# Output layers of a chunked-attention and max-of-three kernel: weights stationary and tokens moving, results stored transposed

## The chip, the cores and the metric

One core of one Trainium2 chip runs the whole program. The metric is the device time of one execution in microseconds (us). TensorE does the matrix products; it holds a stationary operand (128 x 128 in the layers here) and streams a moving operand of 256, 384 or 512 columns through it, adding into PSUM. VectorE (DVE), ScalarE (ACT) and GpSimd (POOL) do the rest, and SyncE (SP) issues every DMA.

## The reference

```python
q, k, v: (8, 8, 576, 64)                       # batch, heads, tokens, width
# attention inside chunks of 64 tokens
scores = (q_c @ k_c^T) / 8
attn = softmax(scores)                          # with 1e-9 added to the sum
x = (attn @ v_c) laid out as (4608, 512)        # tokens by heads*width
h = maximum(maximum(x @ w1, x @ w2), x @ w3)    # w1, w2, w3: (512, 768)
return h @ w_out                                # w_out: (768, 512), result (4608, 512) float32
```

## The kernel before

The 4608 tokens are 36 tiles of 128. Tiles 0 to 7 form two groups of four that are computed plainly; the other 28 are four units of 6, 8, 8 and 6 tiles (`UNITS`, called unit 0 to 3 here). Within a unit, both the hidden layer and the output layer use a seven-product scheme over two-by-two blocks (as Strassen's and Winograd's): products are numbered 1 to 7, and are chained in PSUM as x (1, 6, 5, 3), y (7, 4) and z (2).

Every product in near-float32 precision is three float32r matmuls, `three` (L185 to L188): the stationary and the moving operand are each split into a high and a low half, and it issues low x high, high x low, high x high into one PSUM region. Halves are made by a ScalarE copy (high) and a VectorE subtraction (low). H holds them for the hidden values of a unit (L583 and L586), X for its inputs (L516 and L520).

In the hidden layer (`product`, `hidden`) weights of 128 x 128 from the rings are stationary, and half of the unit's tokens (`half`, 384 or 512 columns) move. The hidden layer goes through nine sets (three pairs of feature blocks by w1, w2, w3). The set's third product is put off into the following set, and that of the last set into the unit's output stage.

The output stage is `project`. For each product in the order `OUT`, and for each of three pairs of feature blocks (`jp`), it goes through the tokens in tiles of 128: the tile's H is stationary, and 256 output columns of the weights move. A PSUM bank takes two tiles of 256 columns. With 3 tiles in half of a 6-tile unit, one bank holds two tiles and a second one holds one. When a product's chain has a result, it is copied aside on ScalarE (L708), added to a kept part on VectorE and stored (L712, L702), or copied on ScalarE and stored (L710, L702). The stores go from four rotating buffers `ao`. Each H is split two products ahead of its use, from within the loop.

The order of the work is written out by a planner: steps of TensorE are yielded one by one with an assumed duration (`OUT_STEP` 0.36 us for three matmuls of 256 columns, `STEP_H` 0.517 or 0.6815 us for three of 384 or 512), and everything else is put into a queue of due times by `plan`, and issued when the assumed clock has passed its time. This fixes the order in which each engine's queue gets its instructions. The inputs X of the next unit are mixed and split (`operands`) from the end of the hidden layer on, at due times that don't depend on the steps of the output stage: behind a 6-tile unit at 9.0 us from the stage's start plus 3.2 us times the entries of `when`, of which 5.0 belongs to `high(3)`. At the ends of products 5 and 4, SyncE is given loads of the next unit's weights.

Of the kernel before, what the change touches and what calls it, by code (L numbers as in the profile page):

```python
# [9 lines left out]
F32 = mybir.dt.float32  # L10
# [9 lines left out]
B, H, S, D = 8, 8, 576, 64  # L20
P = 128
NT = B * S // P
DM, DF, DO = 512, 768, 512
CT, JT = DM // P, DF // P
SCALE = 1.0 / float(D) ** 0.5
GROUPS = [4, 4]
# [6 lines left out]
PAIR_T = (("T", 10.0, 12.4, 0.46), ("at", 10.9, 13.3, 0.0))  # L33
PAIR_D = (("bt", 8.6, 10.5, 0.0), ("bw", 9.6, 11.5, 0.0), ("br", 14.6, 15.6, 0.0))
OUT = (1, 2, 6, 7, 5, 4, 3)
OUT_STEP = 0.36
MIX = 0.5


# [25 lines left out]
def chunk_attn_maxout_kernel(  # L65
# [10 lines left out]
    nc = tc.nc  # L76
# [8 lines left out]
    ao_p = ctx.enter_context(tc.tile_pool(name="ao_p", bufs=1))  # L85
# [15 lines left out]
    def take():  # L101
        assert banks, "no bank is free"
        pool, tag = place = banks.pop(0)
        if not kept_until_read:
            banks.append(place)
        return pool.tile([P, 512], F32, name="pm", tag=tag), place

    def give(place):
        assert kept_until_read
        banks.append(place)  # L110

    ident = small.tile([P, P], F32, name="ident")
    make_identity(nc, ident)

# [11 lines left out]
    for name in FIRST.split():  # L126
        k = (3 * int(name[1]) + int(name[2])) if name[0] in "WAXY" else None
# [57 lines left out]
    def three(o, ah, al, bh, bl, first, last, shared=False):  # L185
        nc.tensor.matmul(out=o, lhsT=al, rhs=bh, start=first, stop=False, skip_group_check=shared)  # L186
        nc.tensor.matmul(out=o, lhsT=ah, rhs=bl, start=False, stop=False, skip_group_check=shared)  # L187
        nc.tensor.matmul(out=o, lhsT=ah, rhs=bh, start=False, stop=last, skip_group_check=shared)  # L188
# [128 lines left out]
    outputs = []  # L317
# [176 lines left out]
    def unit(t0, count, rooms, turn):  # L494


        half = count * 64
        X, ring = {}, {}
        stage, s = rooms["stage"], rooms["s"]
        last_set = len(sets) - 1  # L500

        step = STEP_H[count]
# [56 lines left out]
        chain = {1: "x", 6: "x", 5: "x", 3: "x", 7: "y", 4: "y", 2: "z"}  # L559
# [6 lines left out]
        mixed, H = {}, {}  # L566
# [11 lines left out]
        def split(n, jp):  # L578
            i = OUT[n]

            def high():
                H[i, jp] = hpool.tile([P, 2, 512], F32R, name="H", tag=f"h{n % 2 * 3 + jp}")
                nc.scalar.copy(out=H[i, jp][:, 0, :half], in_=hidden_block(i, jp))  # L583

            def low():
                nc.vector.tensor_tensor(out=H[i, jp][:, 1, :half], in0=hidden_block(i, jp),  # L586
                                        in1=H[i, jp][:, 0, :half].bitcast(F32), op=minus)

            return high, low
# [85 lines left out]
        def of_out(i, jp):  # L675
            if i == 7:
                return [rooms["T3"]()[:, k, jp] for k in range(2)]
            if i in (5, 4):
                return [ring["out", (5, 4).index(i)][:, 3 * k + jp] for k in range(2)]
            j, cols = {1: (2 * jp, slice(0, 256)), 6: (2 * jp, slice(256, 512)), 2: (2 * jp + 1, slice(0, 256)),  # L680
                       3: (2 * jp + 1, slice(256, 512))}[i]
            return [w[:, j, cols] for w in (woh, wol)]

        def project():
            each = count // 2
            groups = [list(range(n, min(n + 2, each))) for n in range(0, each, 2)]
            held = {}

            def kept_out(k, g):
                return s()[:, 2 * k + g, :256 * len(groups[g])]  # L690

            def stores(g, c, d, write, free):
                def fn():
                    outputs.append(0)
                    o = ao_p.tile([P, DO], F32, name="ao", tag=f"ao{len(outputs) % 4}")
                    wide = 256 * len(groups[g])
                    write(o[:, :wide])
                    if free:
                        give(held[free, g][1])
                    first = t0 + c * each + groups[g][0]  # L700
                    rows = out[first * P:(first + len(groups[g])) * P, 256 * d:256 * (d + 1)]
                    nc.sync.dma_start(out=rows.rearrange("(q p) x -> p q x", p=P), in_=o[:, :wide].rearrange("p (q x) -> p q x", x=256))  # L702
                return fn

            def after(i, g):
                o = held[chain[i], g][0]
                if i in (1, 6, 7):
                    return [(0.25, lambda: nc.scalar.copy(out=kept_out(int(i == 6), g), in_=o))]  # L708
                if i == 3:
                    return [(0.25, stores(g, 0, 1, lambda to: nc.scalar.copy(out=to, in_=o), "x"))]  # L710
                c, d, k, free = {2: (0, 0, 0, "z"), 5: (1, 1, 0, None), 4: (1, 0, 1, "y")}[i]
                return [(0.25, stores(g, c, d, lambda to: nc.vector.tensor_tensor(out=to, in0=o, in1=kept_out(k, g), op=plus),  # L712
                                      free))]

            for n, i in enumerate(OUT):
                begins = i in (1, 2, 7)
                if begins:
                    for g, tiles in enumerate(groups):
                        bank, place = take()
                        held[chain[i], g] = bank[:, :256 * len(tiles)], place  # L720
                todo = [(jp, g, q) for jp in range(JT // 2) for g, tiles in enumerate(groups) for q in tiles]
                if n == len(OUT) - 1:
                    todo.sort(key=lambda x: (x[1], x[2]))
                for m, (jp, g, q) in enumerate(todo):
                    cols, to = slice(q * P, (q + 1) * P), slice(q % 2 * 256, q % 2 * 256 + 256)
                    three(held[chain[i], g][0][:, to], H[i, jp][:, 0, cols], H[i, jp][:, 1, cols], *of_out(i, jp),
                          begins and jp == 0 and q % 2 == 0, jp == JT // 2 - 1, True)
                    done = []
                    if jp == JT // 2 - 1 and q == groups[g][-1]:
                        done += after(i, g)  # L730
                    if q == each - 1 and n + 2 < len(OUT) and (n, jp) != (0, 2):
                        done += zip((0.2, 1.1), split(n + 2, jp))
                    if m == len(todo) - 1 and i in (5, 4):
                        done.append((0.1, lambda i=i: rooms["next"](turn + 1, (5, 4).index(i))))
                    yield OUT_STEP, done
                    if n == 0 and jp == 1 and q == each - 1:
                        yield from product(last_set, 3)
                        yield 0.0, [(0.1, lambda: rooms["next"](turn + 1, 2))]

        return dict(operands=operands, load=load, hidden=hidden, project=project, out_weights=out_weights)  # L740

    starts = [sum(GROUPS[:i]) for i in range(len(GROUPS))]
    halves = {}
    def x_tiles(i):
        if i not in halves:
            halves[i] = [xp.tile([P, CT, 512], F32R, name=n, tag=f"{n}{i % 2}") for n in ("xh", "xl")]
        return halves[i]
# [3 lines left out]
    held = {}  # L751

    def hold(name, make):
        if name not in held:
            held[name] = make()
        return held[name]
# [90 lines left out]
    def next_load(u, k):  # L847
# [6 lines left out]
        s=lambda: hold("s", lambda: late["hold"].tile([P, 5, HALF], F32, name="kept")),  # L854
# [3 lines left out]
    g = moe(starts[1], lambda: x_tiles(1))  # L858
    units, t0 = [], sum(GROUPS)
# [110 lines left out]
    with tc.manual_schedule(engines={ET.PE, ET.DVE, ET.Activation, ET.Pool, ET.SP}):  # L970
# [3 lines left out]
        for what, make in parts:  # L974
# [3 lines left out]
            for after in make():  # L978
                step, after = after if isinstance(after, tuple) else (STEP, after)
# [36 lines left out]
```

## Time and profile before

| | |
|---|---|
| median of 3 runs | 620.13 us (619.83 to 622.05) |
| profiled execution | 622.35 us |
| its span, first to last instruction | 620.6 us |
| TensorE busy | 606.5 us, 98% |
| VectorE, ScalarE, GpSimd busy | 424.3, 290.5, 188.6 us |
| TensorE's share of the chain that ended last | 83% |

A matmul's duration in the profile reaches from its issue to its modelled end, and consecutive ones overlap; the pace is the distance of two starts. In a timeline row, what stands in brackets is the engine's idle time before the instruction, and what ended it. The output stages of the four units lie at 254.8 to 280.1, 374.5 to 407.3, 497.4 to 529.1 and 593.5 to 617.4 us.

### The profile page before, as it was taken

How to read it: one execution, taken by the hardware profiler on the slowest of the kernel's cores; microseconds unless marked ns; L12 is line 12 of the kernel's file. 1: busy time of each engine (PE TensorE's matmuls, PEld its weight loads, DVE VectorE, ACT ScalarE, POOL GpSimd, SP SyncE). 2: the span in 40 equal slices, each digit the busy share in tenths (PEclk: the TensorE clock that was granted, in tenths of full speed). 3: DMA queues.
4: the chain of work that ended last, by engine and by line, in shares of the span. 5: the costliest groups of instructions: out<-in, count | busy, mean ns of one | idle time of the engine just before them, and what ended most of it. 6: DMA issues, size and time to landing. Idle time of an engine off the chain costs nothing.

```text
span 620.6 us, 13487 instructions
## 1 busy us (share of the span) xinstructions
PE 606.5 (98%) x5424; PEld 535.7 (86%) x5424; DVE 424.3 (68%) x700; ACT 290.5 (47%) x522; POOL 188.6 (30%) x168
## 2 busy tenths in 40 slices
PE   7899999999999989899999999999999999999997
PEld 3888878887899989897888888988888899999997
DVE  4898965777969954994673769936564597244373
ACT  4887644434365444464343344643333355333343
POOL 2522576786322423300250511002424010031300
PEclk9999999999999999999999999999999999999999
DMA  8988668764969878829786993567758443677532
GB/s 331 373 298 287 222 187 309 255 241 165 363 225 318 295 267 289 299 87 297 261 304 241 327 306 133 167 203 274 257 197 264 166 154 106 221 252 260 196 128 77
DMA packets 62558, 148.99 MB, mean 240 GB/s; under 512 B 5664, under 2 KB 29728, under 8 KB 62496
## 3 DMA queue, kind: packets, MB, share of 16 engines
q1 hardware_dynamic: 62496, 148.13, 68.7%
q8 instruction: 43, 0.70, 0.5%
q14 instruction: 19, 0.16, 0.1%
HBM read 116.92 MB, written 31.20 MB: 239 GB/s over the span
## 4 chain that ended last, share of the span: by engine, by line
PE 83%; DVE 10%; DMA 3%; issue 2%; ACT 1%; POOL 0%; SPq 0%; DVEq 0%; ACTq 0%; POOLq 0%
PE pm L186 26%; PE pm L188 25%; PE pm L187 25%; PE s L236 2%; PE pm L295 2%; DMA ring<-w 2%; DVE e L246 1%; DVE mx L241 1%; PE tp L259 1%; DVE sm L194 1%; PE pm L791 1%; DVE s L427 1%; DVE most L627 1%; DMA out_x<-ao 1%; DVE stage L511 1%
## 5 line engine op out<-in xcount | busy, mean ns | idle before, releaser
L186 PE MATMUL pm<-X,ring 128*128 128x512 f32 (+1 forms) x504 | 185.0, 367 | 5.1 <-ACT kept L618 3.6
L188 PE MATMUL pm<-X,ring 128*128 128x512 f32 (+1 forms) x504 | 182.6, 362 | 0.0
L187 PE MATMUL pm<-X,ring 128*128 128x512 f32 (+1 forms) x504 | 182.4, 362 | 0.0
L618 ACT COPY kept<-pm 128x384 f32<-128x384 f32 (+1 forms) x144 | 76.3, 533 | 129.5 <-PE pm L188 127.5
L186 PEld LDWEIGHTS pm<-X,ring 128*128 128x128 f32 x504 | 94.6, 188 | 17.5 <-ACT kept L618 5.4
L188 PEld LDWEIGHTS pm<-X,ring 128*128 128x128 f32 x504 | 94.6, 188 | 10.2 <-issue 0.3
L187 PEld LDWEIGHTS pm<-X,ring 128*128 128x128 f32 x504 | 94.7, 188 | 9.5
L624 POOL TENSOR_TENSOR kept<-kept 128x384 f32<-128x384 f32 (+1 forms) x24 | 29.8, 1242 | 142.6 <-ACT kept L618 142.6
L621 DVE TENSOR_TENSOR pm<-pm,kept 128x384 f32<-128x384 f32 (+1 forms) x48 | 30.0, 625 | 56.0 <-PE pm L188 56.0
L186 PE MATMUL pm<-xh,wl 128*128 128x512 f32 (+1 forms) x156 | 60.1, 385 | 0.0
L583 ACT CAST H<-most 128x384 fp32r<-128x384 f32 (+1 forms) x72 | 40.5, 567 | 39.1 <-DVE most L627 27.2
L187 PE MATMUL pm<-xl,wh 128*128 128x512 f32 (+1 forms) x156 | 58.4, 374 | 0.3 <-DVE xl L306 0.3
L188 PE MATMUL pm<-xh,wh 128*128 128x512 f32 (+1 forms) x156 | 58.3, 374 | 0.0
L586 DVE TENSOR_TENSOR H<-most,H 128x384 fp32r<-128x384 f32 (+1 forms) x72 | 51.1, 719 | 8.2 <-ACT H L583 7.9
L627 DVE TENSOR_TENSOR most<-pm,most 128x384 f32<-128x384 f32 (+1 forms) x72 | 44.6, 620 | 15.2 <-PE pm L188 13.9
L203 POOL TENSOR_TENSOR e<-e,sm 128x512 f32<-128x512 f32 x27 | 31.9, 1180 | 59.8 <-DVE sm L200 30.0
L624 POOL TENSOR_TENSOR most<-kept 128x384 f32<-128x384 f32 (+1 forms) x12 | 13.8, 1150 | 115.8 <-ACT kept L618 115.8
L186 PE MATMUL pm<-woh,H 128*128 128x256 f32 x168 | 47.6, 283 | 0.3 <-DVE H L586 0.3
L187 PE MATMUL pm<-wol,H 128*128 128x256 f32 x168 | 47.5, 283 | 0.0
L188 PE MATMUL pm<-woh,H 128*128 128x256 f32 x168 | 47.5, 283 | 0.0
L241 DVE TENSOR_REDUCE mx<-s 128x8 f32<-128x512 f32 x36 | 24.6, 683 | 31.2 <-PE s L236 31.2
L520 DVE TENSOR_TENSOR X<-stage,X 128x768 fp32r<-128x768 f32 (+1 forms) x28 | 34.9, 1253 | 12.4 <-ACT X L516 12.1
(119 smaller groups left out, 1143.0 us busy)
## 6 DMA issues: line engine op xcount, KB each, us to landing
ring<-w SPq DMA_DIRECT2D x72, 768.0 KB, 6.2
buf<-in_qk SPq DMA_DIRECT2D x36, 512.0 KB, 6.1
buf<-in_vb SPq DMA_DIRECT2D x36, 256.0 KB, 6.6
ring<-w SPq DMA_DIRECT2D x36, 256.0 KB, 4.1
out_x<-ao SPq DMA_DIRECT2D x32, 256.0 KB, 2.4
w<-s SPq DMA_DIRECT2D x9, 768.0 KB, 4.2
ring<-wo SPq DMA_DIRECT2D x8, 768.0 KB, 6.2
stage<-in_w SPq DMA_DIRECT2D x7, 512.0 KB, 5.5
```

The lines of the kernel that those rows point to most:

```text
L186: nc.tensor.matmul(out=o, lhsT=al, rhs=bh, start=first, stop=False, skip_group_check=shared)
L187: nc.tensor.matmul(out=o, lhsT=ah, rhs=bl, start=False, stop=False, skip_group_check=shared)
L188: nc.tensor.matmul(out=o, lhsT=ah, rhs=bh, start=False, stop=last, skip_group_check=shared)
L203: eng.tensor_tensor(out=e, in0=e, in1=sm.unsqueeze(2).broadcast_to([P, 8, 64]), op=ALU.mult)
L241: nc.vector.tensor_reduce(out=st["mx"].rearrange("p (g c) -> p c g", c=2), in_=st["s"], axis=AX.X, op=ALU.max)
L520: return lambda: eng.tensor_tensor(out=X[i][:, 1], in0=source[i](), in1=X[i][:, 0].bitcast(F32), op=minus)
L583: nc.scalar.copy(out=H[i, jp][:, 0, :half], in_=hidden_block(i, jp))
L586: nc.vector.tensor_tensor(out=H[i, jp][:, 1, :half], in0=hidden_block(i, jp), in1=H[i, jp][:, 0, :half].bitcast(F32), op=minus)
L618: return lambda: nc.scalar.copy(out=to, in_=o)
L621: return lambda: nc.vector.tensor_tensor(out=o if w else M(jp, q), in0=o, in1=kept(k), op=plus)
L624: nc.gpsimd.tensor_tensor(out=kept(3) if w else M(jp, A22), in0=kept(3), in1=kept(p7), op=plus)
L627: return lambda: nc.vector.tensor_tensor(out=M(jp, q), in0=of, in1=M(jp, q), op=most)
```

## The change

In `project`, the operands trade places. A block of 128 output columns of the weights is stationary (two such blocks, `g`, per product), and all tokens of the half move at once, 384 or 512 columns. The PSUM result has output columns on partitions and tokens along the free dimension. It is stored so: the part of `out` behind the first eight tiles is taken as a 512 x 3584 array, and on the host numpy transposes that part when it puts the result together. The assumed duration of a step is that of the hidden layer, and the last product goes through the two blocks one after the other.

```diff
+    plain = sum(GROUPS) * P
+    out_t = out[plain:].rearrange("t x -> (t x)").rearrange("(x t) -> x t", x=DO)
...
-            each = count // 2
-            groups = [list(range(n, min(n + 2, each))) for n in range(0, each, 2)]
...
-                return s()[:, 2 * k + g, :256 * len(groups[g])]
+                return s()[:, 2 * k + g, :half]
...
-                    o = ao_p.tile([P, DO], F32, name="ao", tag=f"ao{len(outputs) % 4}")
-                    wide = 256 * len(groups[g])
-                    write(o[:, :wide])
+                    o = ao_p.tile([P, 512], F32, name="ao", tag=f"ao{len(outputs) % 4}")[:, :half]
+                    write(o)
...
-                    first = t0 + c * each + groups[g][0]
-                    rows = out[first * P:(first + len(groups[g])) * P, 256 * d:256 * (d + 1)]
-                    nc.sync.dma_start(out=rows.rearrange("(q p) x -> p q x", p=P), in_=o[:, :wide].rearrange("p (q x) -> p q x", x=256))
+                    row, col = 256 * d + P * g, (t0 - sum(GROUPS)) * P + c * half
+                    nc.sync.dma_start(out=out_t[row:row + P, col:col + half], in_=o)
...
-                    for g, tiles in enumerate(groups):
+                    for g in range(2):
                         bank, place = take()
-                        held[chain[i], g] = bank[:, :256 * len(tiles)], place
-                todo = [(jp, g, q) for jp in range(JT // 2) for g, tiles in enumerate(groups) for q in tiles]
+                        held[chain[i], g] = bank[:, :half], place
+                todo = [(jp, g) for jp in range(JT // 2) for g in range(2)]
                 if n == len(OUT) - 1:
-                    todo.sort(key=lambda x: (x[1], x[2]))
-                for m, (jp, g, q) in enumerate(todo):
-                    cols, to = slice(q * P, (q + 1) * P), slice(q % 2 * 256, q % 2 * 256 + 256)
-                    three(held[chain[i], g][0][:, to], H[i, jp][:, 0, cols], H[i, jp][:, 1, cols], *of_out(i, jp),
-                          begins and jp == 0 and q % 2 == 0, jp == JT // 2 - 1, True)
+                    todo.sort(key=lambda x: x[1])
+                for m, (jp, g) in enumerate(todo):
+                    hi, lo = (w[:, g * P:(g + 1) * P] for w in of_out(i, jp))
+                    three(held[chain[i], g][0], hi, lo, H[i, jp][:, 0, :half], H[i, jp][:, 1, :half], begins and jp == 0,
+                          jp == JT // 2 - 1, not begins)
...
-                    yield OUT_STEP, done
+                    yield step, done
...
-    return r.results[0]["out_x"]
+    o, plain = np.asarray(r.results[0]["out_x"]), sum(GROUPS) * P
+    return np.concatenate([o[:plain], o[plain:].reshape(DO, -1).T])
```

## Rows read from the trace of the kernel before

**Rows 1.** The page: engines' busy time (share of span), and the granted TensorE clock.

```profile
PE 606.5 (98%) x5424; PEld 535.7 (86%) x5424; DVE 424.3 (68%) x700; ACT 290.5 (47%) x522; POOL 188.6 (30%) x168
...
PEclk9999999999999999999999999999999999999999
```

**Rows 2.** TensorE's groups by shape: first matmul of each three (L187, L188 repeat).

```profile
L186 PE MATMUL pm<-woh,H 128*128 128x256 f32 x168 | 47.6, 283 | 0.3 <-DVE H L586 0.3
...
L186 PE MATMUL pm<-ring,H 128*128 128x256 f32 x84 | 23.8, 283 | 0.0
...
L186 PE MATMUL pm<-T,H 128*128 128x256 f32 x42 | 11.9, 283 | 0.0
```

**Rows 3.** Timeline of TensorE (start, duration): first and last of three even stretches.

```profile
596.74 0.28 PE L186 MATMUL pm<-woh,H 128*128 128x256 f32 x1
...
614.00 0.28 PE L186 MATMUL pm<-woh,H 128*128 128x256 f32 x1
...
574.83 0.33 PE L186 MATMUL pm<-X,ring 128*128 128x384 f32 x1
...
593.37 0.33 PE L188 MATMUL pm<-X,ring 128*128 128x384 f32 x1
...
454.86 0.40 PE L187 MATMUL pm<-X,ring 128*128 128x512 f32 x1
...
486.37 0.39 PE L188 MATMUL pm<-X,ring 128*128 128x512 f32 x1
```

**Rows 4.** Windows of the output stages: length, busy PE, PEld, DVE, ACT, POOL, clock, DMA.

```profile
254.80:280.10 25.30, 24.01 (x197) 23.80 (x196) 25.04 (x43) 13.82 (x28) 1.92 (x2) 1.00 0.46 152
374.50:407.30 32.80, 32.22 (x260) 31.37 (x260) 30.56 (x44) 18.11 (x29) 1.80 (x2) 1.00 0.49 154
497.40:529.10 31.70, 31.70 (x260) 31.40 (x260) 25.62 (x37) 17.66 (x29) 1.80 (x1) 1.00 0.42 131
593.50:617.40 23.90, 23.90 (x197) 23.70 (x195) 15.70 (x30) 11.46 (x24) 1.02 (x1) 1.00 0.34 117
```

**Rows 5.** Timeline of TensorE: where it waits in or behind output stages.

```profile
258.44 0.44 PE L186 MATMUL pm<-X,ring 128*128 128x384 f32 x1 [1.29 <-ACT kept L618]
...
283.79 0.50 PE L186 MATMUL pm<-X,ring 128*128 128x512 f32 x1 [0.77 <-ACT kept L618]
...
377.88 0.50 PE L186 MATMUL pm<-X,ring 128*128 128x512 f32 x1 [0.31 <-ACT kept L618]
...
379.81 0.39 PE L186 MATMUL pm<-woh,H 128*128 128x256 f32 x1 [0.27 <-DVE H L586]
```

**Rows 6.** Timeline of ScalarE around the start of unit 1.

```profile
280.81 0.58 ACT L710 COPY ao<-pm 128x512 f32<-128x512 f32 x1
281.93 0.37 ACT L710 COPY ao<-pm 128x256 f32<-128x256 f32 x1 [0.54 <-DMA out_x<-ao]
282.20 1.05 ACT L516 CAST X<-stage 128x1024 fp32r<-128x1024 f32 x1
283.15 1.08 ACT L618 COPY kept<-pm 128x512 f32<-128x512 f32 x2
```

**Rows 7.** Timeline of VectorE: the last low half of H in unit 0.

```profile
276.41 0.55 DVE L586 TENSOR_TENSOR H<-most,H 128x384 fp32r<-128x384 f32 x1
```

**Rows 8.** The end: last matmul and copy; a 384-column copy; stores by size, time to landing.

```profile
617.12 0.28 PE L188 MATMUL pm<-woh,H 128*128 128x256 f32 x1
...
617.44 0.37 ACT L710 COPY ao<-pm 128x256 f32<-128x256 f32 x1 [0.49 <-PE pm L188]
...
L618 ACT COPY kept<-pm 128x384 f32<-128x384 f32 x72 | 34.2, 479 | 47.4 <-PE pm L188 47.0
...
out_x<-ao SPq DMA_DIRECT2D x32, 256.0 KB, 2.4
...
out_x<-ao SPq DMA_DIRECT2D x8, 128.0 KB, 1.8
...
DMA to landing us min/median/max: 1.7/2.4/6.6
```

More of the change, by code (lines that the diff above doesn't have):

```diff
@@ L35 @@
 OUT = (1, 2, 6, 7, 5, 4, 3)
-OUT_STEP = 0.36
 MIX = 0.5
@@ L717, in project @@
                 if begins:
-                    for g, tiles in enumerate(groups):
+                    for g in range(2):
                         bank, place = take()
-                        held[chain[i], g] = bank[:, :256 * len(tiles)], place
-                todo = [(jp, g, q) for jp in range(JT // 2) for g, tiles in enumerate(groups) for q in tiles]
+                        held[chain[i], g] = bank[:, :half], place
+                todo = [(jp, g) for jp in range(JT // 2) for g in range(2)]
                 if n == len(OUT) - 1:
-                    todo.sort(key=lambda x: (x[1], x[2]))
-                for m, (jp, g, q) in enumerate(todo):
-                    cols, to = slice(q * P, (q + 1) * P), slice(q % 2 * 256, q % 2 * 256 + 256)
-                    three(held[chain[i], g][0][:, to], H[i, jp][:, 0, cols], H[i, jp][:, 1, cols], *of_out(i, jp),
-                          begins and jp == 0 and q % 2 == 0, jp == JT // 2 - 1, True)
+                    todo.sort(key=lambda x: x[1])
[3 more added lines that the diff above has]
+                          jp == JT // 2 - 1, not begins)
                     done = []
-                    if jp == JT // 2 - 1 and q == groups[g][-1]:
+                    if jp == JT // 2 - 1:
                         done += after(i, g)
-                    if q == each - 1 and n + 2 < len(OUT) and (n, jp) != (0, 2):
+                    if g and n + 2 < len(OUT) and (n, jp) != (0, 2):
                         done += zip((0.2, 1.1), split(n + 2, jp))
@@ L734, in project @@
                         done.append((0.1, lambda i=i: rooms["next"](turn + 1, (5, 4).index(i))))
-                    yield OUT_STEP, done
-                    if n == 0 and jp == 1 and q == each - 1:
+                    yield step, done
+                    if n == 0 and jp == 1 and g:
                         yield from product(last_set, 3)
```

## The prediction

> **What bounds the kernel now.** I read the page first: TensorE is busy 98% of the span, its clock is granted in full (2.4 GHz) in every slice, and the other engines are far below [rows 1]. So the time is the number of matmuls times the pace at which they issue, plus the few places where TensorE stands still. The groups by line and shape come second: the units' output layers are 3 x (168 + 84 + 42) = 882 matmuls with 256 moving columns [rows 2]. Third, the timeline of TensorE, because the mean durations of those groups overlap and are no pace. From first to last start: 144 steps at 256 columns in 17.26 us, 0.1199 us each; 107 steps at 384 columns in 18.54 us, 0.1733 each; 139 steps at 512 columns in 31.51 us, 0.2267 each [rows 3]. Last, the windows of the four output stages [rows 4] and the places where TensorE waits in them or just behind them [rows 5]: in units 0 and 1 VectorE is busy nearly all the time (25.04 of 25.30 us, 30.56 of 32.80), in units 2 and 3 it is not.
>
> **The matmuls.** A unit with n tiles has 7 products x 3 pairs of features x n/2 tiles x 3 matmuls of 256 columns: 189 for 6 tiles, 252 for 8. Afterwards it is 7 x 3 x 2 halves of the outputs x 3 = 126 for every unit, of 384 columns (6 tiles) or 512 (8 tiles). The columns are the same in all, 882 x 256 = 252 x 384 + 252 x 512 = 225,792. What goes is 378 matmuls. The rows at 384 and 512 are the hidden layers, of the same three-matmul pattern, with a 128x128 stationary and a float32r moving operand from SBUF, so I use their pace for the new ones:
> - 6 tiles: 189 x 0.1199 - 126 x 0.1733 = 22.66 - 21.84 = 0.82 us less
> - 8 tiles: 252 x 0.1199 - 126 x 0.2267 = 30.21 - 28.56 = 1.65 us less
>
> Two units of each: 4.94 us. The same comes out of the fixed part: 512 less 256 columns is 0.1068 us, so 256 columns of streaming are 0.1068 and 0.0131 us per matmul doesn't depend on the columns; 378 x 0.0131 = 4.95. As bounds for an unseen pairing (this stationary with that moving tile): below, nothing saved, if time went by columns alone; above, 5.0 us. I take 4.94, as rows 3 have the very shapes.
>
> The Trainium skill speaks against that: "TensorE: Matmul & The Clock Gate", section on the back-to-back issue gap, gives N/2.4 + 2.5 ns for a warm matmul, 109, 162.5 and 216 ns at these sizes. By it 378 fewer matmuls are an estimated 0.95 us, and with the tail below the time would be some 619.6. The trace disagrees at all three sizes (119.9, 173.3, 226.7 ns), always by about 11 ns, so its fixed part is five times as large here.
>
> **Unit 0, and the wait behind it.** Two stops in or behind the stage are ended by other engines. At 258.44 TensorE has waited 1.29 us for the ScalarE copy of the last set [rows 5]. That copy depends on work from before the stage, so the 18 x 0.1199 - 12 x 0.1733 = 0.08 us won ahead of it is lost. At 283.79, in the next unit's first set, it has waited 0.77 us for the copy at L618 [rows 5]. ScalarE's queue there is: a store's copy, the second store's copy (held 0.54 us by the landing of an older store out of the same buffer), a cast of X, then L618 [rows 6]. Only if this queue moves does unit 0's gain reach the end. By the planner's own due times it does: counted from the stage's start, the cast (`high(3)`) is due at 9.0 + 3.2 x 5.0 = 25.0, and L618 behind it: 63 steps of 0.36 (22.68), two of 0.517 for the last set's product, two of 0.6815 for the next unit's first product and 0.25 make 25.3. With 42 steps of 0.517 (21.71) in place of the 63, L618 is due at 24.4, ahead of the cast. So L618 could start when the store's copy ends, near 282.35 in place of 283.15: 0.8 us. Bounds: 0 (the landing moves later by as much, since that store grows from 128 to 192 KB) and 1.67 (no wait left: the 0.93 us above the normal step and 0.74 of PE). I take 0.8, which the order supports.
>
> **Unit 1.** The wait before 377.88 is again ended by a copy from before the stage [rows 5], so 24 x 0.1199 - 12 x 0.2267 = 0.15 us is lost there. The one before 379.81 is for the low half of H, which VectorE finishes then. Before, H's low half was the stationary of the first matmul of a three; now the first of the three takes H's high half as moving operand, and the low half is needed by the second. So one matmul (0.23 us) slips in ahead of that wait and the loss is made good. I count the full 1.65. **Unit 2** has no such wait: 1.65.
>
> **Are the operands in time?** H for each product is made two products ahead. The tightest is unit 0's last product: VectorE ends the third block's low half at 276.41 + 0.55 = 276.96 [rows 7]. The product began at 276.87 and its sorted loop needed that block 6 matmuls later, 277.59. Now it begins about 6/7 x 0.82 = 0.7 us earlier, 276.2, but its sixth step is at 6 x 0.1733 = 1.04, 277.2 for the high half, 277.4 for the low: still in time by 0.4, even if VectorE, which is full there, ends no earlier. If that cover went, unit 0 would lose a few tenths.
>
> **Copies and stores.** Per product, two evacuations of 384 columns replace one of 512 and one of 256 in units of 6 (units of 8 keep two of 512). On ScalarE 0.58 + 0.37 [rows 6] becomes 2 x 0.479 [rows 8], nothing either way, VectorE's adds change in the same proportion, and both lie beside TensorE except at the end. The stores stay 32, of the same bytes; pieces of 1 KB become 1.5 or 2 KB, but 14,336 bytes apart. Cost inside the run: none while a buffer of the four is free again in time.
>
> **The tail (unit 3).** Behind the last matmul nothing hides. Its second half was 256 columns [rows 8] and becomes 384: matmul 0.28 to 0.33 (+0.05), copy 0.37 to 0.48 (+0.1), store from 128 KB (1.8 us to landing) to 192 KB, halfway to 256 KB's 2.4 (+0.3) [rows 8]. Together +0.45 (bounds: 0.15 if landing is unchanged, 0.75 at 256 KB's). Unit 3 keeps 0.82 - 0.45 = 0.37.
>
> **Sum.** 0.8 + 1.65 + 1.65 + 0.37 = 4.47 us. The profiled execution took 622.35 us (span 620.6 and 1.75 around it), so 617.9 for it. That execution lies 2.2 above the median of the runs, 620.13; the same 4.47 off the median gives 615.7, 0.72% less. I take half a percent, 3.1 us, as what can be told from no change.
>
> **Rivals.**
> 1. *Units 0 and 1 give their gain back.* For it: VectorE is full there [rows 4] and TensorE already waits for others four times [rows 5]; a faster TensorE may only wait longer. Against it: two of the four waits were priced above at tenths, and the store and the H operands have slack. Then only units 2 and 3 gain, 1.65 + 0.37 = 2.0: 618.1.
> 2. *Time goes by columns.* If the 0.013 us were not per matmul but belonged to the shape of operands, 225,792 columns stay 225,792; the tail's 0.45 remains: 620.6. Against it: three sizes lie on one line [rows 3]. The Trainium skill's page above would put it at 619.6.
> 3. *The transposed stores land late: slower.* Stores now write 128 pieces 14,336 bytes apart. Four buffers rotate, so a store of the fifth product must have landed two products later, 36 x 0.1733 = 6.2 us; after that ScalarE's copy waits, and behind it L618, for which TensorE waits, as at 283.79. With a landing time L the loss is 3 x (L - 6.2) at the units' ends and L - 2.1 in the tail. It eats the 4.94 us from L of about 6.4. At L = 8 it is 5.4 + 5.9 - 4.9 = 6.4 us slower, 626.5. For it: landings of up to 6.6 us occur already [rows 8]. Against it: the median is 2.4 for pieces of half the size, and the largest ones stand behind loads of 768 KB in the same queue.
>
> **How the numbers follow.** Forecast 0.71, rival 1 0.17, rival 2 0.05, rival 3 0.07. Faster by over 0.5% needs 3.1 us: the forecast's cases, with the small part of it that falls short set against the part of rival 1 that loses only one unit: 0.71. Within 0.5%: rivals 1 and 2, 0.22. Slower: 0.07. Range: its fast end is everything kept, with unit 0's wait gone (4.47 + 0.87) and the tail at its lower bound (0.3), and a run's scatter of 0.3: 613.9. Its slow end holds rival 1 with 0.5 of scatter: 618.6. Outside are rivals 2 and 3 and some of the edges.
>
> **What would show it.** In the changed profile: 252 + 252 matmuls on H at steps of 0.173 and 0.227 us; output stages of about 0.8 us (6 tiles) or 1.6 us (8 tiles) less; the wait before the next unit's L618 no longer than 0.8 us and L618 ahead of the cast; the last store landing near 2.1 us. Wrong: steps on H longer than those of X; waits on H in the last product of units 0 or 1; landings of out_x beyond 6 us; ScalarE waiting for out_x in every unit.

## The result and the profile after

The changed kernel takes 615.86 us (median of 6 runs, 615.46 to 617.59), the kernel before 621.75 beside it (median of 6, 619.83 to 622.94). The ratio is 0.9916, with a 95% interval of 0.9894 to 0.9939: 3.8 to 6.6 us less. The forecast was 615.7. The profiled execution took 617.24 us, 5.11 less than the profiled one of before; its span went from 620.58 to 615.46.

The groups by shape, first matmul of each three (operands of the output layers; the other two lines of a three repeat the counts): where [rows 2] had 882 matmuls of 256 columns, there are 3 x (48 + 24 + 12) = 252 of each new size.

```profile
L187 PE MATMUL pm<-H,wol 128*128 128x512 f32 x48 | 18.7, 389 | 0.0
...
L187 PE MATMUL pm<-H,wol 128*128 128x384 f32 x48 | 16.0, 334 | 0.0
...
L187 PE MATMUL pm<-H,ring 128*128 128x512 f32 x24 | 9.3, 389 | 0.0
...
L187 PE MATMUL pm<-H,ring 128*128 128x384 f32 x24 | 8.0, 334 | 0.0
...
L187 PE MATMUL pm<-H,T 128*128 128x512 f32 x12 | 4.7, 389 | 0.0
L187 PE MATMUL pm<-H,T 128*128 128x384 f32 x12 | 4.0, 334 | 0.0
```

Their pace, from TensorE's timeline (start, duration). In unit 2, 113 steps from 498.67 to 524.28: 0.2267 us each. In unit 3, 113 steps from 592.13 to 611.72: 0.1733 us each. Both are the pace of the hidden layer in [rows 3], to the fourth digit.

```profile
498.67 0.39 PE L187 MATMUL pm<-H,wol 128*128 128x512 f32 x1
...
524.28 0.39 PE L189 MATMUL pm<-H,woh 128*128 128x512 f32 x1
...
592.13 0.33 PE L187 MATMUL pm<-H,wol 128*128 128x384 f32 x1
...
611.72 0.34 PE L189 MATMUL pm<-H,woh 128*128 128x384 f32 x1
```

The windows of the output stages (length, then busy PE, PEld, DVE, ACT, POOL, clock, DMA), beside [rows 4]. TensorE's clock is still granted in full, and VectorE is as full in units 0 and 1 as it was.

```profile
254.40:279.10 24.70, 23.34 (x135) 23.02 (x134) 24.43 (x43) 13.53 (x27) 1.97 (x2) 1.00 0.48 153
373.40:404.50 31.10, 30.62 (x134) 24.69 (x134) 29.74 (x44) 17.95 (x29) 1.79 (x2) 1.00 0.51 167
494.50:524.60 30.10, 30.10 (x135) 24.92 (x134) 25.57 (x37) 17.56 (x29) 1.81 (x1) 1.00 0.44 143
589.00:612.10 23.10, 23.05 (x133) 22.73 (x132) 15.20 (x30) 11.66 (x25) 1.01 (x1) 1.00 0.34 124
```

Where the span's 5.12 us went, by the starts of TensorE's instructions at the edges of the stages:

| stretch | before | after | difference |
|---|---|---|---|
| up to unit 0's output stage | 254.84 | 254.49 | -0.35 |
| unit 0, output stage | 25.27 | 24.54 | -0.73 |
| unit 1, hidden layer | 94.43 | 94.41 | -0.02 |
| unit 1, output stage | 32.73 | 31.00 | -1.73 |
| unit 2, hidden layer | 90.17 | 90.15 | -0.02 |
| unit 2, output stage | 31.61 | 29.92 | -1.69 |
| unit 3, hidden layer | 64.49 | 64.51 | +0.02 |
| unit 3, output stage, to the start of its last matmul | 23.58 | 22.71 | -0.87 |
| from there to the end | 3.46 | 3.74 | +0.28 |

The first line has nothing of the change in it: over the twelve profiles of this study the start of that stage lies anywhere between 252.4 and 254.8 us. A good part of this is TensorE's waiting for weights (`ring<-w`) in unit 0's hidden layer: 1.51 us in the kernel before, 0.64 + 0.93 in the changed one, none in four of the others. So lengths of stages are compared below, and times of whole runs only where the difference is over 2 us. Output stages of the same work repeat to within 0.1 us; unit 1's hidden layer to 0.3 us.

The places where TensorE waits, as in [rows 5]:

```profile
258.09 0.44 PE L187 MATMUL pm<-X,ring 128*128 128x384 f32 x1 [1.36 <-ACT kept L619]
...
282.41 0.50 PE L187 MATMUL pm<-X,ring 128*128 128x512 f32 x1 [0.45 <-ACT kept L619]
...
375.94 0.39 PE L189 MATMUL pm<-H,woh 128*128 128x512 f32 x1
376.77 0.50 PE L187 MATMUL pm<-X,ring 128*128 128x512 f32 x1 [0.44 <-ACT kept L619]
377.11 0.39 PE L188 MATMUL pm<-X,ring 128*128 128x512 f32 x1
...
378.26 0.39 PE L187 MATMUL pm<-H,wol 128*128 128x512 f32 x1
378.69 0.50 PE L188 MATMUL pm<-H,woh 128*128 128x512 f32 x1
379.03 0.40 PE L189 MATMUL pm<-H,woh 128*128 128x512 f32 x1
```

Each row is as forecast: the waits inside the stages grew by what was won ahead of them (1.29 to 1.36, 0.31 to 0.44), and at 378.26 one matmul on H's high half goes before the pause for the low half. At 282.41 the wait is shorter, and ScalarE's timeline around it shows why: of the casts and copies in [rows 6], L619 at 281.75 now stands ahead of the cast of 282.23.

```profile
281.01 0.85 ACT L707 COPY ao<-pm 128x384 f32<-128x384 f32 x2
281.75 0.60 ACT L619 COPY kept<-pm 128x512 f32<-128x512 f32 x1
282.23 1.07 ACT L517 CAST X<-stage 128x1024 fp32r<-128x1024 f32 x1
```

### The profile page after: what moved, and what is told of

Its sections match the earlier page's. It is cut to its first block, busy times and chain, and to the rows that moved or that the text cites. A ratio compares the mean times of both kernels' runs of the same rounds, so it can differ in the third digit from the quotient of the medians.

```text
span 615.5 us, 12717 instructions
## 1 busy us (share of the span) xinstructions
PE 601.4 (98%) x5046; PEld 520.5 (85%) x5046; DVE 424.0 (69%) x700; ACT 290.7 (47%) x522; POOL 188.9 (31%) x168
## 4 chain that ended last, share of the span: by engine, by line
PE 79%; DVE 12%; DMA 3%; issue 2%; ACT 1%; SPq 1%; POOL 0%; DVEq 0%; ACTq 0%; POOLq 0%
PE pm L187 24%; PE pm L188 24%; PE pm L189 24%; DMA ring<-w 3%; PE pm L296 2%; PE s L237 2%; DVE H L587 1%; DVE e L247 1%; DVE X L521 1%; DVE sm L195 1%; PE tp L260 1%; DVE stage L512 1%; DVE mx L242 1%; PE pm L788 1%; DVE s L428 1%
## 5 line engine op out<-in xcount | busy, mean ns | idle before, releaser
L187 PE MATMUL pm<-X,ring 128*128 128x512 f32 (+1 forms) x504 | 185.2, 367 | 5.2 <-ACT kept L619 3.6
L188 PE MATMUL pm<-X,ring 128*128 128x512 f32 (+1 forms) x504 | 182.4, 362 | 0.0
L619 ACT COPY kept<-pm 128x384 f32<-128x384 f32 (+1 forms) x144 | 76.6, 534 | 128.0 <-PE pm L189 126.1
L187 PEld LDWEIGHTS pm<-X,ring 128*128 128x128 f32 x504 | 94.6, 188 | 18.4 <-ACT kept L619 5.9
L188 PEld LDWEIGHTS pm<-X,ring 128*128 128x128 f32 x504 | 94.7, 188 | 9.6
L187 PE MATMUL pm<-xh,wl 128*128 128x512 f32 (+1 forms) x156 | 60.1, 385 | 0.0
L188 PE MATMUL pm<-xl,wh 128*128 128x512 f32 (+1 forms) x156 | 58.4, 374 | 0.3 <-DVE xl L307 0.3
L587 DVE TENSOR_TENSOR H<-most,H 128x384 fp32r<-128x384 f32 (+1 forms) x72 | 49.6, 702 | 7.1 <-ACT H L584 6.7
L517 ACT CAST X<-stage 128x768 fp32r<-128x768 f32 (+1 forms) x28 | 26.2, 943 | 26.2 <-DVE stage L512 20.0
L251 ACT ACTIVATE e<-e 128x512 f32<-128x512 f32 x36 | 22.8, 633 | 31.7 <-DVE e L247 31.7
L188 PE MATMUL pm<-H,woh 128*128 128x384 f32 (+1 forms) x96 | 34.8, 363 | 0.0
```

The source lines that it names most:

```text
L619: return lambda: nc.scalar.copy(out=to, in_=o)
```

## The experiments

Line numbers in these kernels are those of the changed kernel unless a row shows others.

**Weights stationary, but 256 columns again (8-tile units).** Is it the number of matmuls, or which operand moves?

```diff
-                    three(held[chain[i], g][0], hi, lo, H[i, jp][:, 0, :half], H[i, jp][:, 1, :half], begins and jp == 0, ...)
+                    for at in [range(n, n + 256) for n in (0, 256)] if count == 8 else [range(half)]:
+                        c = slice(at.start, at.stop)
+                        three(held[chain[i], g][0][:, c], hi, lo, H[i, jp][:, 0, c], H[i, jp][:, 1, c], ...)
```

> The changed kernel, but in the two 8-tile units the tokens move in two pieces of 256 columns: weights stay stationary and results stay transposed, but units 1 and 2 are back at 252 output matmuls of 256 columns each, the number and size of the kernel before. Theory A (a fixed 0.013 us per matmul): the matmuls on H there step by 0.120 us, the output stages of units 1 and 2 grow by 252 x 0.1199 - 126 x 0.2267 = 1.65 us each, from 31.00 and 29.92 to about 32.6 and 31.6; the time is 3.3 us above the changed kernel's, near 619 us. Rival (the exchanged roles or the transposed results are what saves): stages stay at 31.0 and 29.9, the time stays near 616.

Measured: 619.0 us (0.9968 of before, 0.9954 to 0.9982). Stages of units 1 and 2: 32.58 and 31.61 us, the latter the kernel before's own to the hundredth. The windows of these two stages:

```profile
371.90:404.50 32.60, 32.16 (x259) 31.38 (x258) 30.73 (x44) 18.05 (x29) 1.77 (x2) 1.00 0.52 163
494.60:526.30 31.70, 31.70 (x261) 31.40 (x260) 25.70 (x37) 17.60 (x29) 1.81 (x1) 1.00 0.44 140
```

From 500.01 to 526.17 there are 218 steps in unit 2, 0.1200 us each:

```profile
500.01 0.28 PE L187 MATMUL pm<-H,wol 128*128 128x256 f32 x1
...
526.17 0.28 PE L189 MATMUL pm<-H,woh 128*128 128x256 f32 x1
```

So in unit 2, which has no waits, the exchanged roles are worth nothing by themselves; the number of matmuls is all. The 0.15 us that unit 1 stays below the kernel before (32.73) are of its waits.

**192 columns (6-tile units).** How far down does the line of fixed part and columns hold?

```diff
+                    for at in [range(n, n + 192) for n in (0, 192)] if count == 6 else [range(half)]:
```

> The changed kernel, but in the two 6-tile units the tokens move in two pieces of 192 columns: 252 output matmuls in each instead of 126. Theory A (a fixed 0.0131 us and 0.000417 us per column): a step of 0.093 us, 23.5 us in place of 21.8, units 0 and 3 grow by 1.6 us each, the time is near 619. Rival (a floor from the loading of the stationary operand, as the transposes with 128 moving columns already step by 0.109 us): a step of 0.109 us or more, 27.5 us, units 0 and 3 grow by 5.6 us each, the time is near 627.

Measured: 626.98 us (1.0100 of before, 1.0085 to 1.0115). The rival holds: it steps by 0.1117 us (146 steps in 16.30 us), not 0.093, and units 0 and 3 take 30.20 and 29.06 us, 5.7 and 6.4 more (in unit 0 the wait for L619 shrinks from 1.36 to 0.77 us meanwhile).

```profile
605.10 0.27 PE L187 MATMUL pm<-H,wol 128*128 128x192 f32 x1
...
621.40 0.27 PE L189 MATMUL pm<-H,woh 128*128 128x192 f32 x1
```

A line fitted to 256, 384 and 512 columns is no rule for 192.

**128 columns (6-tile units).** A floor, or a price for the cut?

```diff
+                    for at in [range(n, n + 128) for n in (0, 128, 256)] if count == 6 else [range(half)]:
```

> The changed kernel, but in the two 6-tile units the tokens move in three pieces of 128 columns: 378 output matmuls in each. The run with 192 columns stepped by 0.111 us, where the line of the other sizes gives 0.093. Theory A (below some 235 columns a step is set by something that doesn't depend on the columns, the loading of the stationary operand): a step of 0.107 to 0.112 us, output stages of about 40.5 to 42.5 us plus 1.0 for the hidden layer's product in them. Rival (the pieces' start at odd places of a bank or of H costs some 0.018 us each, on top of the line): 0.0131 + 128 x 0.000417 + 0.018 = 0.085 us, stages near 33 us.

Measured: 654.48 us (one run). A step is 0.1117 us again (170 steps in 18.98 us), with a third fewer columns. Output matmuls of the two sizes, by form, first the kernel with 128 and then the one with 192; the mean durations are equal too:

```profile
L187 PE MATMUL pm<-H,wol 128*128 128x128 f32 x144 | 39.4, 274 | 0.0
```

```profile
L187 PE MATMUL pm<-H,wol 128*128 128x192 f32 x96 | 26.2, 273 | 0.0
```

So there is a floor of 0.1117 us per matmul, each with its load of a 128x128 float32r stationary. The stages are 43.2 and 43.1 us, as the floor gives; the rival's 33 is far off. The start of unit 0's stage, with the loads (PEld), says more of the cause:

```profile
252.63 0.22 PE L187 MATMUL pm<-H,wol 128*128 128x128 f32 x1
252.63 0.19 PEld L188 LDWEIGHTS pm<-H,woh 128*128 128x128 f32 x1
252.69 0.27 PE L188 MATMUL pm<-H,woh 128*128 128x128 f32 x1
252.74 0.19 PEld L189 LDWEIGHTS pm<-H,woh 128*128 128x128 f32 x1
252.80 0.27 PE L189 MATMUL pm<-H,woh 128*128 128x128 f32 x1
```

The first step is 0.06 us: the second matmul's load began together with the first matmul. From then on a load begins 0.05 us behind the start of a matmul, and loads and matmuls alike come every 0.11 us. With 192 columns the first step is 0.09 us, and the loads then come every 0.11 us as well. So the columns alone don't make the floor. That the load does is likely, but no run leaves the loads out.

**The planner's old clock.** Did the order on ScalarE carry unit 0's gain across?

```diff
-                    yield step, done
+                    yield 0.09 * count, done
```

> The changed kernel, but the planner is told the old duration of the output stage (0.54 and 0.72 us per step in place of 0.517 and 0.6815), so that the queues get their order from the old clock: on ScalarE the copy L619 of the next unit's first product stands behind the cast high(3) again. Theory A (the swap of these two is what carried unit 0's gain into unit 1): the wait in unit 1's first set grows from 0.45 us by 0.4 to 0.8 us, all else within 0.2 us of the changed kernel, the time 0.4 to 0.8 us more. Rival (the order doesn't matter, the copy waits for the store's landing): the wait stays at 0.45 us within 0.1.

Measured: 616.21 us (0.9923, 0.9908 to 0.9938), which by itself tells nothing. In the trace the cast is back ahead of L619, and TensorE waits 1.08 us for it in place of 0.45:

```profile
280.21 0.48 ACT L707 COPY ao<-pm 128x384 f32<-128x384 f32 x1 [0.27 <-DMA out_x<-ao]
280.59 1.05 ACT L517 CAST X<-stage 128x1024 fp32r<-128x1024 f32 x1
281.53 1.08 ACT L619 COPY kept<-pm 128x512 f32<-128x512 f32 x2
```

```profile
282.18 0.50 PE L187 MATMUL pm<-X,ring 128*128 128x512 f32 x1 [1.08 <-ACT kept L619]
```

Unit 1's hidden layer takes 94.83 us, 0.42 more; all output stages are the same to 0.02. The order is worth 0.4 to 0.6 us, by the stretch (which itself repeats only to 0.3) and by the wait. It isn't all: TensorE goes on behind this wait 28.95 us after the stage's start in the kernel before, 28.54 with the old clock and 27.92 in the changed kernel. So of 1.03 us, 0.62 come with the order and 0.41 without it.

**One VectorE mix later.** What are the waits inside the stages of units 0 and 1?

```diff
-            return [..., (-3.5, low(7)), (-2.0, t2(nc.vector))] + [
+            return [..., (-3.5, low(7)), (first - 1.3, t2(nc.vector))] + [
```

> The changed kernel, but one VectorE operation, the mix t2 for the next unit's X (L512, 2.07 us in unit 0 and 1.47 us in unit 1), is due behind the middle of the output stage rather than just ahead of it. Theory A (the waits of 1.36 and 0.44 us for L619 inside the output stages of units 0 and 1 come from work that stands ahead of the stage in VectorE's queue): these two waits go or shrink to under 0.3 us, the stages of units 0 and 1 shrink by 1.0 to 1.4 and 0.4 to 0.7 us, and the time falls by 1.3 to 2.0 us to near 614. Rival (VectorE is full in units 0 and 1 and what leaves one place comes back in another): a wait for H in the last products of units 0 or 1 takes its place, the time stays within 0.5 us.

Measured: 615.43 us (0.9911, 0.9896 to 0.9926). The mix now begins 9.7 us into unit 0's stage and 13.3 us into unit 1's, so ahead of the middle and not behind it, and takes 1.22 us in both. Both waits are gone, but the two units answer differently, and neither by the forecast amount. Unit 1's stage falls by 1.07 us (0.4 to 0.7 forecast) to 29.92, exactly that of unit 2. Unit 0's falls by only 0.34 (1.0 to 1.4 forecast), since another wait comes in, and the one in unit 1's first set grows:

```profile
273.81 0.41 PE L187 MATMUL pm<-H,wol 128*128 128x384 f32 x1 [0.73 <-DVE ao L709]
...
280.86 0.50 PE L187 MATMUL pm<-X,ring 128*128 128x512 f32 x1 [0.59 <-ACT kept L619]
```

and unit 1's hidden layer gives back 0.30 (94.71). So theory A holds in unit 1, and something like the rival in unit 0: the new wait is for an add (L709), not for H. On VectorE, that add stands behind another mix:

```profile
271.97 1.22 DVE L512 TENSOR_TENSOR stage<-stage 128x1024 f32<-128x1024 f32 x1
273.11 0.55 DVE L709 TENSOR_TENSOR ao<-pm,kept 128x384 f32<-128x384 f32 x1
```

That mix begins 18.8 us into the stage, as in the changed kernel (19.0), while TensorE arrives earlier: VectorE's queue didn't move with it. How full VectorE is doesn't tell the units apart (23.34 of 24.20 us in unit 0, 29.22 of 30.00 in unit 1).

**float32r in the idle matmuls.** Whose is the fixed part? (Their results are not used.)

```diff
-    idle = hpool.tile([P, 512], mybir.dt.bfloat16, name="h", tag="h5")
+    idle = hpool.tile([P, 512], F32R, name="h", tag="h5")
```

> The changed kernel, but the 26 idle matmuls at the start (128x512, always the same stationary, results unused) take float32r operands in place of bfloat16. In bfloat16 they step by 0.216 us at full clock, 0.011 less than the 512-column matmuls of the layers. Theory A (most of the fixed 0.013 us per matmul belongs to the float32r format): the idle matmuls step by 0.226 to 0.228 us at full clock. Rival (it belongs to the change of the stationary operand or of the tiles): they stay at 0.216. The time of the whole within 1 us of the changed kernel's, but for their few steps.

Measured: 614.94 us (one run). The timeline merges a burst; two bursts of 5 and 8, first of the changed kernel (bfloat16), then with float32r:

```profile
6.94 1.25 PE L788 MATMUL pm<-h 128*128 128x512 bf16 x5
...
9.17 1.90 PE L788 MATMUL pm<-h 128*128 128x512 bf16 x8
```

```profile
6.64 1.42 PE L788 MATMUL pm<-h 128*128 128x512 f32 x5
...
8.87 2.11 PE L788 MATMUL pm<-h 128*128 128x512 f32 x8
```

Three matmuls more take 0.65 us in bfloat16, 0.217 each, and 0.69 in float32r, 0.230 each; their single steps lie between 0.224 and 0.236, a bit above the expected 0.228. So with one and the same stationary, float32r costs 0.013 us more per matmul than bfloat16: the fixed part goes with the format. TensorE loads the stationary again before each of them, and whether the 0.013 us go with these loads (188 against 98 ns each in these bursts) or with the stream isn't separated. It is one run.

**Contiguous stores.** Do rows 14,336 bytes apart cost anything?

```diff
-                    nc.sync.dma_start(out=out_t[row:row + P, col:col + half], in_=o)
+                    nc.sync.dma_start(out=out_flat[at:at + P * half].rearrange("(p x) -> p x", x=half), in_=o)
```

> The changed kernel, but every store of a unit's result goes into one contiguous block of out (128 rows of 1.5 or 2 KB one behind the other) rather than into 128 pieces 14,336 bytes apart; numpy puts the blocks in place. Theory A (the transposed stores cost nothing inside the run, and in the tail only by their size): landing times within 0.2 us of the changed kernel's, last store 1.8 us, the time within 1 us of the changed kernel's 616. Rival (scattered rows slow the stores, and some of the gain is lost to it): landings shorter by over 0.5 us, the wait of 0.45 us in unit 1's first set goes, the time falls by 0.5 us or more.

Measured: 616.27 us (0.9933, 0.9917 to 0.9949). Landings by size (median us in the last column), first of the changed kernel, then with contiguous blocks; the wait in unit 1 is 0.46 us, and the output stages are those of the changed kernel to 0.07 us. The stores' addresses cost nothing that shows.

```profile
out_x<-ao SPq DMA_DIRECT2D x24, 256.0 KB, 2.8
out_x<-ao SPq DMA_DIRECT2D x16, 192.0 KB, 1.8
```

```profile
out_x<-ao SPq DMA_DIRECT2D x24, 256.0 KB, 2.6
out_x<-ao SPq DMA_DIRECT2D x16, 192.0 KB, 1.8
```

**Low half first.** Did one matmul really slip in ahead of the wait for H?

```diff
...
+        nc.tensor.matmul(out=o, lhsT=ah, rhs=bl, start=first, stop=False, skip_group_check=shared)
+        nc.tensor.matmul(out=o, lhsT=al, rhs=bh, start=False, stop=False, skip_group_check=shared)
         nc.tensor.matmul(out=o, lhsT=ah, rhs=bh, start=False, stop=last, skip_group_check=shared)
```

> The changed kernel, but in the output stages the three matmuls of a step come in another order: the one that needs the low half of H as moving operand is first. Theory A (in the changed kernel one matmul slips in ahead of the wait for the low half of H in unit 1): a wait of 0.2 to 0.3 us for VectorE comes back there, and unit 1's stage grows from 30.99 us by 0.1 to 0.25; the other stages stay within 0.05 us. Rival (the order makes no difference, the wait shrank because VectorE came earlier): unit 1's stage stays at 31.0.

Measured (one run): the wait is back, unit 1's stage is 31.24 us, 0.24 longer, and the other stages are within 0.04. (The time, 616.85, holds another wait of 0.73 us, for a load in unit 1's hidden layer.)

```profile
378.08 0.50 PE L192 MATMUL pm<-H,woh 128*128 128x512 f32 x1 [0.26 <-DVE H L592]
```

**Put together, with a split last copy.**

```diff
-            ... (-2.0, t2(nc.vector))] + [
+            ... (first - 1.3 if first > 9.0 else -2.0, t2(nc.vector))] + [
...
+                        nc.scalar.copy(out=to[:, :half // 2], in_=o[:, :half // 2])
+                        nc.vector.tensor_copy(out=to[:, half // 2:], in_=o[:, half // 2:])
```

> The changed kernel with two edits: the mix t2 is due late only behind the 8-tile units (unit 0, where its move only brought a new wait of 0.73 us, keeps the old place), and the last evacuation is split between ScalarE and VectorE, 192 columns each. Theory A: unit 0's stage 24.5 us, unit 1's 29.9 (1.07 less), unit 2's 29.9, the tail 3.6 us in place of 3.74, together 1.2 us less than the changed kernel, near 614.5. Rival (unit 1's gain comes back as a longer wait in unit 2, as it did behind unit 0): the stretch from unit 1's stage to unit 2's grows from 90.15 us by 0.3 or more, and the time is within 0.7 us of the changed kernel's.

Measured: 614.8 us (0.9910, 0.9894 to 0.9926). Stages of units 0 to 2 as expected (24.51, 29.92, 29.92, and 90.17 between the last two), but the tail is 3.91 us, longer by 0.17. VectorE's half is ended by ScalarE's, so the two run one after the other:

```profile
610.03 0.32 ACT L708 COPY ao<-pm 128x192 f32<-128x192 f32 x1 [1.08 <-PE pm L189]
```

```profile
610.38 0.36 DVE L709 COPY ao<-pm 128x192 f32<-128x192 f32 x1 [2.92 <-ACT ao L708]
```

0.32 + 0.36 is more than the 0.48 of one copy. The split is a miss. Both halves read one PSUM bank and write one tile `ao`; which of the two holds VectorE back isn't separated.

**The same without the split.**

```diff
-            ... (-2.0, t2(nc.vector))] + [
+            ... (first - 1.3 if first > 9.0 else -2.0, t2(nc.vector))] + [
```

> The changed kernel with one edit: the mix t2 is due late behind the 8-tile units alone; the last evacuation is whole again on ScalarE. Theory A (the split's 0.17 us came from VectorE's half waiting for ScalarE's half of the same bank): the tail is back at 3.74 us, the output stages are 24.5, 29.9, 29.9 and 22.7 us, the time 0.17 us less than with the split and about 1.1 less than the changed kernel's, near 614.7. Rival (the tail moved for another reason, such as the moved mix): the tail stays at 3.9.

Measured: 615.93 us (613.55 to 617.46; 0.9921 of before, 0.9900 to 0.9942). The tail is 3.74 us again, the stages 24.52, 29.92, 29.92 and 22.71, all as expected; the time is not (614.7 expected). By its stages this kernel is 1.1 us better than the changed one, but the times don't tell the two apart (0.9921 and 0.9916): the scatter ahead of unit 0 is larger than the gain. So it beats the kernel before, and only in the trace the changed one.

## Why the prediction was right, point by point

- **The matmuls.** Forecast 0.82 us per 6-tile unit and 1.65 per 8-tile unit. Measured in the undisturbed units: 0.87 and 1.69. The pace was taken from the hidden layer's rows of the very shapes, and the changed kernel runs at it to the fourth digit. The run with 256 columns shows the step itself: with the number of matmuls back, the gain of units 1 and 2 is gone (all of it in unit 2, all but 0.15 us in unit 1). So rival 2, by which time goes by columns, is refuted for these sizes.
- **The Trainium skill's figure.** The Trainium skill's fixed 2.5 ns per matmul ("TensorE: Matmul & The Clock Gate", back-to-back issue gap) would have made it an estimated 0.95 us. It does hold for the idle bfloat16 matmuls (0.217 us at 512 columns) and not for the float32r ones of the layers; the measurement decides.
- **Unit 0.** Forecast: 0.08 of 0.82 lost at a wait set by earlier work, and 0.8 carried into unit 1 by the new order on ScalarE. Measured: stage 0.73 less, L619 ahead of the cast, wait 0.45 in place of 0.77. The hidden layer behind it didn't grow, which is all that the gain needed. Up to the end of that wait 1.03 us are won, more than the 0.8 forecast, but by the end of the hidden layer only 0.75 are left. The difference lies within the scatter of that stretch: kernels with the same work and the same wait there (0.44 to 0.46 us) take 94.12, 94.24, 94.41 and 94.43 us.
- **Unit 1.** 0.15 lost at one wait and more than made good at the next: the prediction's own terms, 1.65 - 0.15 + 0.23, give the 1.73 measured, where it counted 1.65. The order of the three is shown to be worth 0.24.
- **Operands and stores.** No new wait on H and none on stores. Rival 3 (late stores) is refuted twice: the landings are those of contiguous blocks, and though up to 7.2 us occur (largest in the trace, 6.6 before), no stage became longer by them. Landings beyond 6 us were named as a sign of being wrong, and four came: it was no sign, as such landings were there before. All four are among the last three stores of a unit, whose buffers are next written over 20 us later, in the next unit's hidden layer. The buffer of unit 0's last copy was free in time, but by 0.4 us only: the store from it landed at 281.02, and the copy began at 281.38.
- **Rival 1** (units 0 and 1 give their gain back) didn't come about, but it was near: with the planner's old clock 0.4 to 0.6 us of unit 0's gain are lost, and with one VectorE operation moved into unit 0's stage a new wait of 0.73 us comes in.
- **The tail** was mis-sized: 0.45 forecast, 0.28 measured. The last matmul (+0.05) and copy (+0.11) are as counted, but the last store, of 192 KB, lands in 1.82 us where that of 128 KB took 1.70: 0.12 more, and not 0.3. The prediction also has the last matmul's 0.05 twice, in the tail and in 189 steps against 126; up to the start of the last matmul 0.87 are gained, not 0.82.
- **Sum.** 4.47 forecast, 5.12 in the profile: 0.35 of the difference lies ahead of unit 0 and is scatter, 0.17 is the tail, and 0.13 the units. From unit 0's output stage on, 4.77 us are gained.
- **The number.** That 615.86 came so near to 615.7 is luck: the kernel before took 621.75 beside it and not the 620.13 that the forecast was taken off, and the start of unit 0's stage alone scatters by 2.4 us. The range's fast end is mis-added: its terms, 4.47 + 0.87 + 0.3 + 0.3 off 620.13, give 614.2 and not 613.9; the result lies inside either.

The tail, matmul, copy and landings, beside [rows 8]. The last copy and, from all 32 stores, the times to landing:

```profile
612.09 0.48 ACT L707 COPY ao<-pm 128x384 f32<-128x384 f32 x1 [1.08 <-PE pm L189]
```

```profile
DMA to landing us min/median/max: 1.8/2.1/7.2
```

## What to carry to other kernels

Where TensorE is the bound, take its pace at each size from the starts in the timeline, split it into a part per column and a part per matmul, and choose as moving the operand that fills more columns, up to the 512 here; then count what is left of the matmuls. Check next what each engine's queue holds at the stage's edges: a gain in one stage reaches the end only if the copy that the next stage waits for moves too, and the order that a planner gives may decide that. A mean over whole runs could not see effects of 0.3 to 1 us here; lengths of stages could.

## What the runs showed of the hardware

- A float32r matmul on a 128x128 stationary steps by 0.0131 us + 0.000417 per column at 256, 384 and 512 columns, but in a stream by 0.1117 us at 192 and at 128 columns alike. By an estimate from these numbers the two meet near 237 columns. Cutting the moving operand to 192 or 128 columns costs 5.7 to 20.4 us per unit here.
- A good 0.01 us of the fixed part goes with the format: 0.217 us at 512 columns in bfloat16, 0.230 in float32r, both with an unchanged stationary (one run).
- A 512-column matmul behind a wait is followed by a first step of 0.34 us in place of 0.227, and the idle time in brackets counts from the modelled end of the matmul before, 0.39 us behind its start and not 0.227. So a wait costs some 0.27 us more than stands in its brackets. The two waits in unit 1's stage, 0.44 and 0.04 us in the rows above, are steps of 0.83 and 0.43 us in place of 0.227, each followed by one of 0.34: together 1.03 us, which is what the stage lost when they went (1.07).
